# RWKV attention and a two-level mixture of experts: the routing's prefix product one step later, own bytes for the first part's buffers, the decay loaded as rows

## The chip, the cores and the metric

The kernel runs on one core of one Trainium2 chip, one launch. The metric is the device time of that core in microseconds (us). Engines are named as the profile names them: PE is TensorE's matmul stream and PEld its weight loads, DVE is VectorE, ACT is ScalarE, POOL is GpSimd, SP only issues DMAs here. "PEclk" or "clock" is the granted TensorE clock as a share of 2.4 GHz; it has two levels, 1.0 (2.4 GHz) and 0.5 (1.2 GHz).

## What is computed

Four batches of 8 heads, 768 positions, head size 48, all float32. First a linear recurrence over positions (RWKV), then every token goes to one of 16 experts in 4 groups of 4:

```python
for t in range(S):
    kt, vt, rt = k[:, :, t], v[:, :, t], r[:, :, t]
    cur = einsum('bhd,bhe->bhde', u * kt, vt)
    y[:, :, t] = einsum('bhd,bhde->bhe', rt, state + cur)
    state = w * state + einsum('bhd,bhe->bhde', kt, vt)
x = y.transpose(0, 2, 1, 3).reshape(3072, 384)
g_logits = x @ w_group;  g_idx = argmax(g_logits);  g_w = softmax(g_logits)[g_idx]
e_logits = x @ w_expert[g_idx];  e_idx = argmax(e_logits);  e_w = softmax(e_logits)[e_idx]
out = (g_w * e_w) * (relu(x @ w1[g_idx, e_idx]) @ w2[g_idx, e_idx])
```

## The kernel before

There are two parts that follow each other on PE: the recurrence with the routing, and the experts.

**First part.** The 768 positions are cut into 6 chunks of 128, so there are 24 tiles (chunk c, batch b), tile n = 4c + b, and 12 pairs of tiles g = n // 2. `load_pair` (L317) brings k, r and v of a pair from DRAM on SP's queue. A table of powers of the decay is built first (L125 to L158): `wc` from the loaded decay, four scans, a reciprocal, T1T, a transposition and a flip on PE, and T2. Then a software pipeline of steps s = 0 to 27 runs (L443), each step emitting for different tiles:

- `turn(s)` (L346): PE transposes r (`pr`) and scaled k (`pk`); DVE makes rT, ACT copies kT.
- `scores(s-1)` (L358): 8 products `pa` on PE, masked by DVE into `am`.
- `values(s-2)` (L372): products `py` and, except in the last chunk, `pu` on PE; DVE adds into `xt` and updates the state R (one operation in the first chunk, `ts` and R later).
- `rows_T(s-3)` (L411): PE transposes xt (`px`), ACT copies. `row_logits(s-4)` (L416): the routing's logits `pl` on PE, copied by ACT into `lg`.
- POOL: `scale_k` (L328, kh = k times T2) in even steps, `own` (L331, two products dg) in odd ones; DVE turns dg into the tile's own term in `own_values` (L337) in odd steps.

After tiles 3, 7, 11, 15 and 19 four tiles are routed together (the last four tiles as 2, 1 and 1). `route` (L202) gives four pieces: `choice` (DVE: maxima, one-hot `ohe`, running counts `cum`), `before` (PE: a prefix product `pre` of ohe with a triangle, and of cum with ones), `place_and_gate` (DVE) and `rows` (POOL: an indirect DMA of 128 rows into the expert's region of `x_sorted`). For tile n, emitted at the end of step s = n + 4, choice and before come in step s + 1 behind `rows_T` and ahead of `row_logits`, place_and_gate in s + 2, and one rows piece in each step from s + 2 on.

The order of PE, DVE, ACT and POOL is that of emission (`manual_schedule`, L434); each engine takes its instructions strictly in that order. SP's order is chosen by the scheduling framework. Tiles of a released pool give their bytes to later tiles, which then wait for the last use: the pool "powers" (L125) is released before "ring" and "wkv" (L299) are opened. PSUM has 8 banks given out in turn by `bank` (L74).

In step 2, ahead of its turn, come `late_constants` (L180: small DVE operations, some on one partition) and `zero_places` (L195: two DMAs of 2.7 MB each, issued from ACT's queue, that clear the regions). In step 4 both first experts' weights are asked for (L452).

**Second part** (L505 on): for each of 16 experts, 224 rows are read back from x_sorted, turned, multiplied by w1 and w2 on PE and written out by POOL. Nothing in it is changed.

Of the kernel before, what the change touches and what calls it, by code (L numbers as in the profile page):

```python
# [15 lines left out]
P = 128  # L16
# [10 lines left out]
def kernel(  # L27
# [58 lines left out]
    wcol = cst([P, HP], "wcol")  # L86
    nc.vector.memset(wcol, 1.0)
    for e in range(2):
        nc.scalar.dma_start(out=wcol[DP * e : DP * e + D, :], in_=w.rearrange("(a e) d -> e d a", e=2)[e])
# [6 lines left out]

    gw = cst([P, KO, NL], "gw")
    nc.scalar.dma_start(out=gw[:, :, 0:G], in_=moe_w_group.rearrange("(ko p) g -> p ko g", p=P))
    for g in range(G):
        nc.scalar.dma_start(  # L100
            out=gw[:, :, G + Eg * g : G + Eg * (g + 1)], in_=moe_w_expert[g].rearrange("(ko p) e -> p ko e", p=P)
        )
# [16 lines left out]
    )  # L119

# [4 lines left out]
    with tc.tile_pool(name="powers", bufs=1) as pw:  # L125

        wc = pw.tile([P, HP], FP32, name="wc")
        nc.vector.tensor_scalar(out=wc, in0=wcol, scalar1=W_LEAST, scalar2=W_MOST, op0=OP.max, op1=OP.min)
        none = pw.tile([P, P], FP32, name="none")
        nc.vector.memset(none, 0.0)  # L130

        up_to = pw.tile([P, HP, P], FP32, name="up_to")
        for hc in range(HP):
            nc.vector.tensor_tensor_scan(
                up_to[:, hc, :], wc[:, hc : hc + 1].to_broadcast([P, P]), none, 1.0, OP.mult, OP.add
            )
        by = pw.tile([P, HP], FP32, name="by")
        nc.vector.reciprocal(by, up_to[:, :, 64])
        for hc in range(HP):
            nc.vector.tensor_scalar(  # L140
                out=T1T[:, hc, :], in0=up_to[:, hc, :], scalar1=by[:, hc : hc + 1], scalar2=None, op0=OP.mult
            )
        ptab = bank([P, HP, P], "ptab")
        for hc in range(HP):
            nc.tensor.transpose(ptab[:, hc, :], T1T[:, hc, :], ident)
        tab = pw.tile([P, HP, P], FP32, name="tab")
        nc.scalar.copy(tab, ptab)
        ptab2 = bank([P, HP, P], "ptab2")
        nc.tensor.matmul(
            ptab2.rearrange("p a b -> p (a b)"), lhsT=flip, rhs=tab.rearrange("p a b -> p (a b)"), start=True, stop=True  # L150
        )
        nc.scalar.copy(
            T2.rearrange("p (a e) d -> p a e d", e=2), ptab2.rearrange("p a (e d) -> p a e d", e=2)[:, :, :, 0:D]
        )
        nc.vector.memset(WLm, 0.0)
        for e in range(2):
            rows = slice(DP * e, DP * e + D)
            nc.vector.tensor_copy(WLm[rows, :, D * e : D * (e + 1)], up_to[rows, :, P - 1 : P].to_broadcast([D, HP, D]))  # L158
# [10 lines left out]
    nc.vector.memset(nothing, 0.0)  # L169
# [9 lines left out]

    def late_constants():  # L180
# [4 lines left out]
        nc.vector.tensor_copy(cum[:, 0, :], start0)  # L185

# [8 lines left out]
    def zero_places():  # L195

        regions = xs_dram.rearrange("(e n) w -> n e w", e=GE)
        half = CAP // 2
        for j in range(2):
            nc.scalar.dma_start(out=regions[half * j : half * (j + 1)], in_=spread(nothing[0:half, :], 1, GE))  # L200

    def route(pool, lg, xt, T, sums, number, group):  # L202
# [43 lines left out]
        def place_and_gate():  # L246
            at = tl([P, T, GE], "at")
            nc.vector.tensor_mul(at, held["pre"], ohf)
            place = tl([P, T], "place")
            nc.vector.reduce_sum(out=place, in_=at, axis=AX)  # L250
            nc.vector.tensor_copy(place_i, place)
# [10 lines left out]

        def rows(i):
# [35 lines left out]
    with tc.tile_pool(name="ring", bufs=1) as ring, tc.tile_pool(name="wkv", bufs=2) as pool:  # L299
        R = [ring.tile([P, HP, 2 * D], FP32, name=f"R_{b}") for b in range(B)]  # L300
        RING = 4
        NP = NT // 2
        rts = [ring.tile([P, 2, H, DP], FP32, name=f"rt_{j}") for j in range(RING)]
        khs = [ring.tile([P, 2, H, DP], FP32, name=f"kh_{j}") for j in range(RING)]

        tiles = [(c, b) for c in range(NCH) for b in range(B)]
        kts, vts, dgs, dvs = {}, {}, {}, {}
        rkT, ams, xts, lgs, xTs = {}, {}, {}, {}, {}

        def load(src, g, dst):  # L310
            c, b0 = g // (B // 2), 2 * (g % (B // 2))
            nc.sync.dma_start(
                out=dst.rearrange("p a h d -> p (a h) d"),
                in_=src[b0 : b0 + 2, :, P * c : P * (c + 1), :].rearrange("b h t d -> t (b h) d"),
            )

        def load_pair(g):  # L317

            kts[g] = pool.tile([P, 2, H, D], FP32, tag="kt", bufs=3, name="kt")
            vts[g] = pool.tile([P, 2, H, D], FP32, tag="vt", bufs=5, name="vt")  # L320
            if g < RING:
                nc.vector.memset(rts[g][:, :, :, D:DP], 0.0)
                nc.vector.memset(khs[g][:, :, :, D:DP], 0.0)
            load(k, g, kts[g])
            load(r, g, rts[g % RING][:, :, :, 0:D])
            load(v, g, vts[g])

        def scale_k(g):  # L328
            nc.gpsimd.tensor_mul(khs[g % RING][:, :, :, 0:D], kts[g], spread(T2, 1, 2))  # L329

        def own(g):  # L331

            dg = dgs[g] = pool.tile([P, 2, H, D], FP32, tag="dg", name="dg")
            nc.gpsimd.tensor_mul(dg, rts[g % RING][:, :, :, 0:D], kts.pop(g))  # L334
            nc.gpsimd.tensor_mul(dg, dg, spread(ub, 1, 2))

        def own_values(g):  # L337
            du = pool.tile([P, 2, H], FP32, tag="du", name="du")
            nc.vector.reduce_sum(out=du, in_=dgs.pop(g), axis=AX)  # L339
            dv = dvs[g] = pool.tile([P, 2, H, D], FP32, tag="dv", bufs=3, name="dv")  # L340
            nc.vector.tensor_mul(dv, vts[g], spread(du, 3, D))
# [4 lines left out]
        def turn(n):  # L346
            g, a = n // 2, n % 2
            pr, pk = bank([P, HP, P], "pr"), bank([P, HP, P], "pk")
            for dst, src in ((pr, rts[g % RING]), (pk, khs[g % RING])):
# [22 lines left out]
        def values(n):  # L372
            c, b = tiles[n]
            g, a = n // 2, n % 2
            vt, kh = vts[g], khs[g % RING]
# [13 lines left out]
            if b == 0:  # L389
                xts[c] = pool.tile([P, B, XW], FP32, tag="xt", bufs=4, name="xt")  # L390
# [43 lines left out]
        engines = {mybir.EngineType.PE, mybir.EngineType.DVE, mybir.EngineType.Activation, mybir.EngineType.Pool}  # L434
        with tc.manual_schedule(engines=engines):
            load_pair(0)
            numbers()
            scale_k(0)
            load_pair(1)
            own(0)  # L440
            last_step = NT + 3
            todo = {}
            for s in range(last_step + 1):  # L443

                pieces = todo.pop(s, [])
# [13 lines left out]
                if 0 <= s - 1 < NT:  # L459
                    scores(s - 1)  # L460
# [354 lines left out]
```

## Time and profile before

| | us |
|---|---|
| median of 3 runs | 613.65 |
| lowest, highest | 612.9, 628.15 |
| the profiled execution, its own time | 611.63 |
| its span, first to last instruction | 609.9 |
| mean granted TensorE clock in it | 0.851 |
| PE busy | 549.3 (90%) |
| DVE busy | 187.3 (31%) |
| ACT busy | 85.6 (14%) |
| POOL busy | 126.5 (21%) |

How to read it: PE at half clock is as "busy" as at full clock, so the clock stands beside the busy share wherever it matters. A timeline row gives start, duration, engine, line, operation, what is written from what, the count of instructions merged into the row and, in brackets, how long the engine was idle before it and what released it. Durations of merged rows are from the first start to the last end, and matmuls' ends are modelled. "ACTq" and "SPq" rows are DMA issues: the time that the engine's queue spent on issuing.

### The profile page before, as it was taken

To read this page: it belongs to the slowest core of one execution; us is meant where nothing else is said; L and a number is where in the kernel's file an instruction comes from. 1 tells how busy PE (TensorE), PEld (TensorE's weight loads), DVE (VectorE), ACT (ScalarE), POOL (GpSimd) and SP (SyncE) were. 2 spreads that over 40 slices of the span, in tenths; PEclk is the share of its full clock that TensorE was granted. 3 is DMA by queue.
4 is the path that set the end of the run, shared out by engine and by line. 5 is a ranking of instruction groups with operands and counts; after the bars stand their busy time and mean duration, and the time that the engine had idled before them with its cause. 6 is when DMAs were issued, how large, how long until landed. Compare 5 with 4: busy or idle time off the path is not lost. (4 is left out here: it accounts for less than half of the span.)

```text
span 609.9 us, 7907 instructions
## 1 busy us (share of the span) xinstructions
PE 549.3 (90%) x3264; PEld 532.2 (87%) x3264; DVE 187.3 (31%) x484; ACT 85.6 (14%) x195; POOL 126.5 (21%) x102
## 2 busy tenths in 40 slices
PE   2679969899899899872999999999999999999993
PEld 0679859799799799872999999999999999999993
DVE  3576665742653643353011011111111011110100
ACT  1101101101110110110111111111111111111110
POOL 1836135505404311023010011101111011100111
PEclk9959967955955855555999999999999999999998
DMA  9999995523101001005246566564746556454200
GB/s 148 245 294 286 291 176 104 104 53 92 40 0 40 14 13 40 1 29 166 106 148 226 178 218 194 182 224 156 245 149 216 192 187 228 149 202 144 105 21 23
DMA packets 110989, 85.83 MB, mean 141 GB/s; under 512 B 78855, under 2 KB 102541, under 8 KB 110946
## 3 DMA queue, kind: packets, MB, share of 16 engines
q1 hardware_dynamic: 97344, 64.49, 40.1%
q10 hardware_dynamic: 10274, 11.30, 5.7%
q0 software_dynamic: 3328, 9.47, 4.5%
q8 instruction: 27, 0.44, 0.3%
q14 instruction: 16, 0.13, 0.1%
HBM read 70.25 MB, written 15.78 MB: 141 GB/s over the span
## 5 line engine op out<-in xcount | busy, mean ns | idle before, releaser
L543 PE MATMUL ph<-xe,w 128*128 128x224 f32 x768 | 152.2, 355 | 1.0 <-DVE xe L524 1.0
L556 PE MATMUL po<-hT,w 128*128 128x224 f32 x768 | 150.7, 353 | 0.0
L543 PEld LDWEIGHTS ph<-xe,w 128*128 128x128 f32 x768 | 145.4, 192 | 1.7 <-DVE xe L524 1.4
L556 PEld LDWEIGHTS po<-hT,w 128*128 128x128 f32 x768 | 144.2, 190 | 0.0
L573 POOL DMA_INDIRECT out_dram<-yt,ids x32 | 30.6, 957 | 292.7 <-DVE yt L568 287.8
L385 PE MATMUL py<-vt,am 128*128 128x48 f32 x384 | 71.6, 327 | 0.0
L385 PEld LDWEIGHTS py<-vt,am 128*128 128x128 f32 x384 | 69.1, 256 | 0.6 <-issue 0.2
L568 DVE TENSOR_SCALAR yt<-pb,gates 128x384 f32<-128x384 f32 (+1 forms) x32 | 18.2, 611 | 167.0 <-PE pb L566 167.0
L547 ACT ACTIVATE hT<-ph 128x448 f32<-128x448 f32 x64 | 34.8, 544 | 137.8 <-PE ph L543 137.8
L265 POOL DMA_INDIRECT x_sorted<-xt,place_i x24 | 24.2, 1007 | 122.3 <-DVE xt L261 117.8
L380 PE MATMUL py<-R,rT 128*128 128x96 f32 x160 | 46.0, 380 | 0.0
L365 PE MATMUL pa<-rT,kT 48*128 48x128 f32 x384 | 40.5, 370 | 4.6 <-DVE rT L353 4.6
L365 PEld LDWEIGHTS pa<-rT,kT 48*128 48x128 f32 x384 | 34.9, 266 | 10.5 <-issue 8.9
L370 DVE TENSOR_TENSOR am<-pa,later 128x512 f32<-128x512 f32 x48 | 30.9, 684 | 34.5 <-PE pa L365 34.5
L380 PEld LDWEIGHTS py<-R,rT 128*128 128x128 f32 x160 | 33.5, 259 | 3.2 <-issue 2.0
L559 ACT COPY yT<-po 128x224 f32<-128x224 f32 x48 | 16.6, 346 | 134.8 <-PE po L556 112.0
L524 DVE COPY xe<-px 128x448 f32<-128x448 f32 (+1 forms) x32 | 14.7, 502 | 65.0 <-PE px L521 65.0
L290 ACT COPY xT<-px 128x384 f32<-128x384 f32 x24 | 11.5, 480 | 152.4 <-PE px L289 152.4
L334 POOL TENSOR_TENSOR dg<-rt,kt 128x768 f32<-128x768 f32 x12 | 25.1, 2093 | 28.4 <-DVE du L339 20.8
L329 POOL TENSOR_TENSOR kh<-kt,T 128x768 f32<-128x768 f32 x12 | 21.9, 1829 | 32.1 <-DMA kt<-in_k_dram 19.9
L295 PEld LDWEIGHTS pl<-gw,xT 128*128 128x128 f32 x144 | 28.4, 286 | 0.0
L400 PE MATMUL pu<-vt,kh 128*128 128x96 f32 x160 | 28.2, 332 | 0.0
(93 smaller groups left out, 408.1 us busy)
## 6 DMA issues: line engine op xcount, KB each, us to landing
w<-in_moe_w_dram SPq DMA_DIRECT2D x32, 1536.0 KB, 6.5
x_sorted<-nothing ACTq DMA_DIRECT2D x2, 2702.0 KB
kt<-in_k_dram SPq DMA_DIRECT2D x12, 384.0 KB, 4.9
vt<-in_v_dram SPq DMA_DIRECT2D x12, 384.0 KB, 7.2
rt<-in_r_dram SPq DMA_DIRECT2D x12, 384.0 KB, 6.7
xg<-x_sorted ACTq DMA_DIRECT2D x16, 193.0 KB, 3.5
xg<-x_sorted ACTq DMA_DIRECT2D x16, 144.8 KB, 3.6
out_dram<-yt,ids POOLq DMA_INDIRECT x32, 2.5
```

The costliest lines, as they stand in the source:

```text
L265: ins = nc.gpsimd.indirect_dma_start(out=xs_dram, out_offset=bass.IndirectOffsetOnAxis(ap=place_i[:, i : i + 1], axis=0), in_=xt[:, i, :], ...
L295: nc.tensor.matmul(pl, lhsT=xT[:, ko, :], rhs=gw[:, ko, :], start=(ko == 0), stop=(ko == KO - 1))
L334: nc.gpsimd.tensor_mul(dg, rts[g % RING][:, :, :, 0:D], kts.pop(g))
L365: nc.tensor.matmul(pa[e][:, hc, :], lhsT=kT[rows, hc, :], rhs=rT[rows, hc, :], start=True, stop=True, skip_group_check=True,)
L370: nc.vector.tensor_mul(am[:, e], pa[e], spread(later, 1, HP))
L380: nc.tensor.matmul(py[:, hc, :], lhsT=rT[:, hc, :], rhs=R[b][:, hc, :], start=True, stop=False, skip_group_check=True,)
L385: nc.tensor.matmul(py[:, hc, D * e : D * (e + 1)], lhsT=am[:, e, hc, :], rhs=vt[:, a, 2 * hc + e, :], start=(c == 0), stop=True, skip_grou ...
L400: nc.tensor.matmul(pu[:, hc, :], lhsT=heads(kh, a, hc), rhs=heads(vt, a, hc), start=True, stop=True, skip_group_check=True,)
L543: nc.tensor.matmul(ph[:, i, :], lhsT=w1[:, ko, P * (f + i) : P * (f + i + 1)], rhs=xe[:, ko, :], start=(ko == 0), stop=(ko == KO - 1), ski ...
L547: nc.scalar.activation(hTs[e][:, f : f + 2, :], ph, AF.Relu)
L556: nc.tensor.matmul(po, lhsT=w2[:, fo, P * d : P * (d + 1)], rhs=hT[:, fo, :], start=(fo == 0), stop=(fo == FO - 1))
L573: ins = nc.gpsimd.indirect_dma_start(out=out, out_offset=bass.IndirectOffsetOnAxis(ap=ids, axis=0), in_=yt, in_offset=None, bounds_check=N ...
```

## The change

The change does these things:

1. **Routing.** `before` of the four-tile routings is emitted first thing in step s + 2, ahead of that step's turn; choice stays in s + 1. So `row_logits` of step s + 1 now stands ahead of `before` on PE. `place_and_gate` is split in two, gate first, then place.
2. **Bytes.** The pools "powers" and "ring" are gone: powers, ring, R, k and v tiles have bytes of their own in `const`. To make room, kh has 3 buffers (4 before), rT 3 (4), xt 3 (4), dv 2 (3); k has 4 (3).
3. **Head.** The decay is loaded as 4 partitions of contiguous rows (`w2h`) on SP's queue and turned by PE (`pw`), in place of two DMAs of single elements on ACT's queue. Loads come in the order r, k, v, and SP too is in the order of emission. A small ACT copy is put ahead of the table's. `scale_k(0)` is made half by DVE and half by POOL. The padding of the other ring tiles is cleared by POOL, in the head, not by DVE in steps. The gate weights `gw` (5 DMA issues on ACT) come behind T2, not ahead. WLm is made at the end of step 0.
4. **Steps.** `late_constants` moves to the end of step 2 and takes a memset; `zero_places` is split over steps 3 and 6; the first two experts' weights are asked for in steps 12 and 20; `scale_k` moves from even steps to the odd ones, just ahead of `own`.

The diff, cut to its core:

```diff
-    for e in range(2):
-        nc.scalar.dma_start(out=wcol[DP * e : DP * e + D, :], in_=w.rearrange("(a e) d -> e d a", e=2)[e])
+    rts = [cst([P, 2, H, DP], f"rt_{j}") for j in range(RING)]
+    khs = [cst([P, 2, H, DP], f"kh_{j}") for j in range(RING - 1)]
+    kts = [cst([P, 2, H, D], f"kt_{j}") for j in range(RING)]
+    vts = [cst([P, 2, H, D], f"vt_{j}") for j in range(RING + 1)]
+    nc.sync.dma_start(out=w2h[:, :, 0:D], in_=w.rearrange("(a e) d -> a e d", e=2))
...
+        load(r, g, rts[g % RING][:, :, :, 0:D])
+        load(k, g, kts[g % RING])
+        load(v, g, vts[g % (RING + 1)])
...
+    nc.scalar.copy(none[:, 0:1], ones[:, 0:1])
...
+    nc.tensor.transpose(pw, w2h.rearrange("p e d -> p (e d)"), ident[0:HP, 0:HP])
+    nc.vector.tensor_scalar(out=wc, in0=pw, scalar1=W_LEAST, scalar2=W_MOST, op0=OP.max, op1=OP.min)
...
     def late_constants():
...
+        nc.vector.memset(nothing, 0.0)
...
-        return choice, before, place_and_gate, rows
+        return choice, before, gate, place, rows
...
-            rT = pool.tile([P, HP, P], FP32, tag="rT", bufs=4, name="rT")
+            rT = pool.tile([P, HP, P], FP32, tag="rT", bufs=3, name="rT")
...
+        def piece_list(n):
+            choice, before, gate, place, rows = routing(n)
+            T = ROUTED[n]
+            if n >= NT - B:
+                lags = [0] * (4 + T)
+            else:
+                lags = [1, 2, 2, 2] + [3 + i for i in range(T)]
+            parts = [choice, before, gate, place] + [lambda i=i: rows(i) for i in range(T)]
+            return [(lag, part is before and lag > 0, part) for lag, part in zip(lags, parts)]
+        numbers()
+        scale_k(0, nc.vector, 0, 1)
+        scale_k(0, nc.gpsimd, 1, 2)
+        for t in rts[1:] + khs[1:]:
+            nc.gpsimd.memset(t[:, :, :, D:DP], 0.0)
+        load_small()
+        load_pair(1)
+        own(0)
...
+            if s in (3, 6):
+                zero_places(s // 6)
+            if s in (12, 20):
+                early[s // 20] = load_expert(s // 20)
+            for first, part in pieces:
+                if first:
+                    part()
             if s < NT:
                 turn(s)
-                    if s % 2 == 0 and s // 2 + 1 < NP:
-                        scale_k(s // 2 + 1)
-                    if s % 2 == 1 and s // 2 + 1 < NP:
-                        own(s // 2 + 1)
+                if s % 2 == 1 and s // 2 + 1 < NP:
+                    scale_k(s // 2 + 1, nc.gpsimd)
+                    own(s // 2 + 1)
...
+            for first, part in pieces:
+                if not first:
+                    part()
+            if s == 0:
+                state_decay()
+            if s == 2:
+                late_constants()
```

## Rows read from the trace of the kernel before

**Rows 1.** The page, part 2: TensorE's clock in 40 equal slices of the span, in tenths.
```profile
PEclk9959967955955855555999999999999999999998
```
**Rows 2.** Stretches between changes of clock: start:end, length, then busy time (instructions) of each engine, PEclk.
```profile
45.80:79.90 34.10, 29.31 (x287) 27.79 (x283) 23.61 (x36) 5.45 (x13) 15.76 (x9) 1.00 1.17 277
79.90:100.40 20.50, 18.60 (x99) 17.59 (x99) 10.31 (x26) 2.27 (x6) 3.38 (x3) 0.50 1.00 141
100.40:120.80 20.40, 17.99 (x171) 16.95 (x169) 15.11 (x28) 2.96 (x7) 14.32 (x9) 1.00 0.56 113
120.80:151.60 30.80, 30.61 (x163) 29.14 (x162) 11.80 (x28) 3.52 (x9) 8.49 (x6) 0.50 0.31 69
...
209.60:291.50 81.90, 65.34 (x320) 61.69 (x320) 32.10 (x137) 7.26 (x22) 11.74 (x12) 0.50 0.14 46
291.50:609.90 318.40, 309.03 (x1714) 307.05 (x1712) 37.10 (x110) 51.45 (x112) 30.61 (x32) 0.99 0.50 167
```
**Rows 3.** Timeline of PE: scores of tiles 6, 7, then 12 and 13.
```profile
63.22 1.16 PE L365 MATMUL pa<-rT,kT 48*128 48x128 f32 x16
...
69.88 1.16 PE L365 MATMUL pa<-rT,kT 48*128 48x128 f32 x16
...
124.63 2.08 PE L365 MATMUL pa<-rT,kT 48*128 48x128 f32 x16
...
137.23 2.08 PE L365 MATMUL pa<-rT,kT 48*128 48x128 f32 x16
```
**Rows 4.** Timeline around the prefix products of steps 8 and 12.
```profile
77.22 1.99 POOL L335 TENSOR_TENSOR dg<-dg,ub 128x768 f32<-128x768 f32 x1
77.73 1.58 DVE L223 TENSOR_TENSOR key<-lg,mx 128x80 f32<-128x80 f32 x1
...
81.80 0.69 PE L237 MATMUL pre<-ohe,later 128*128 128x64 f32 x2 [6.69 <-DVE ohe L229]
...
119.03 0.24 DVE L223 TENSOR_TENSOR key<-lg,mx 128x80 f32<-128x80 f32 x1
...
120.40 0.44 PE L237 MATMUL pre<-ohe,later 128*128 128x64 f32 x2 [2.41 <-DVE ohe L229]
...
121.50 1.41 PE L295 MATMUL pl<-gw,xT 128*128 128x20 f32 x6
```
**Rows 5.** Timeline of steps 2 to 4: late constants, scores of tiles 2 and 3.
```profile
30.48 2.04 DVE L189 TENSOR_TENSOR wlim<-wlim,wrow 1x384 f32<-1x384 f32 x1
...
34.19 2.58 PE L365 MATMUL pa<-rT,kT 48*128 48x128 f32 x16 [4.56 <-DVE rT L353]
...
44.41 1.78 PE L365 MATMUL pa<-rT,kT 48*128 48x128 f32 x16
```
**Rows 6.** Timeline of the head, from the first operations to the scores of tile 1.
```profile
0.90 0.24 POOL L172 IOTA iota_f<- 128x128 f32 x1 [0.40 <-POOLq L801]
...
3.49 4.43 ACTq L100 DMA_DIRECT2D gw<-in_moe_w_expert_dram  x4
...
7.42 0.17 DVE L128 TENSOR_SCALAR wc<-wcol 128x4 f32<-128x4 f32 x1 [5.36 <-DMA wcol<-in_w_dram]
...
13.62 0.48 ACT L152 COPY T<-ptab 128x384 f32<-128x384 f32 x1 [2.23 <-PE ptab L149]
...
18.61 1.82 POOL L334 TENSOR_TENSOR dg<-rt,kt 128x768 f32<-128x768 f32 x1 [2.62 <-DMA rt<-in_r_dram]
...
24.74 1.16 PE L365 MATMUL pa<-rT,kT 48*128 48x128 f32 x16
```
**Rows 7.** Timeline of the end of the first part: scores of tiles 22, 23, first rows of the last routings.
```profile
237.08 2.08 PE L365 MATMUL pa<-rT,kT 48*128 48x128 f32 x16
...
246.14 2.08 PE L365 MATMUL pa<-rT,kT 48*128 48x128 f32 x16
...
270.32 0.98 POOL L265 DMA_INDIRECT x_sorted<-xt,place_i  x1 [39.41 <-DVE xt L261]
```
**Rows 8.** The page, part 6: DMA issues, KB each, median us from issue to landing.
```profile
x_sorted<-xt,place_i POOLq DMA_INDIRECT x24, 2.8
```

More of the change, by code (lines that the diff above doesn't have):

```diff
@@ L95 @@
     nc.scalar.dma_start(out=wrow, in_=bass.AP(tensor=w.tensor, offset=w.offset, ap=[[0, 1], [1, H * D]]))
[L97 to L102, printed above, removed]
+    load_pair(0)
     ones = cst([P, P], "ones")
@@ L119 @@
     )
+    none = cst([P, P], "none")
+    nc.vector.memset(none, 0.0)
+    nc.scalar.copy(none[:, 0:1], ones[:, 0:1])
+    nc.vector.memset(none[:, 0:1], 0.0)
     T1T = cst([P, HP, P], "T1T")
@@ L124 @@
     WLm = cst([P, HP, 2 * D], "WLm")
[L125 to L135, printed above, removed]
-            )
[L137 to L158, printed above, removed]
@@ new lines @@
+    ptab = bank([P, HP, P], "ptab")
+    for hc in range(HP):
+        nc.vector.tensor_scalar(
+            out=T1T[:, hc, :], in0=up_to[:, hc, :], scalar1=by[:, hc : hc + 1], scalar2=None, op0=OP.mult
+        )
+        nc.tensor.transpose(ptab[:, hc, :], T1T[:, hc, :], ident)
+    tab = cst([P, HP, P], "tab")
+    nc.scalar.copy(tab, ptab)
+    ptab2 = bank([P, HP, P], "ptab2")
+    nc.tensor.matmul(
+        ptab2.rearrange("p a b -> p (a b)"), lhsT=flip, rhs=tab.rearrange("p a b -> p (a b)"), start=True, stop=True
+    )
@@ L178, in numbers, with state_decay @@
         nc.gpsimd.iota(region, pattern=[[RG, GE]], base=0, channel_multiplier=0, allow_small_or_imprecise_dtypes=True)
+    def state_decay():
+        nc.vector.memset(WLm, 0.0)
+        for e in range(2):
+            rows = slice(DP * e, DP * e + D)
+            nc.vector.tensor_copy(WLm[rows, :, D * e : D * (e + 1)], up_to[rows, :, P - 1 : P].to_broadcast([D, HP, D]))
     def late_constants():
@@ L244, in before, with gate @@
             )
[L246 to L251, printed above, removed]
+        def gate():
             sx = tl([P, T, NA], "sx")
@@ new lines @@
+        scale_k(0, nc.gpsimd, 1, 2)
[4 more added lines that the diff above has]
+        own(0)
+        todo = {}
+        early = {}
+        for s in range(NT + 4):
+            if s == NT + 2:
+                for t in sorted(todo):
+                    for _, part in todo.pop(t):
+                        part()
+            pieces = todo.pop(s, [])
+            if s % 2 == 0 and s // 2 + 2 < NP:
+                load_pair(s // 2 + 2)
+            if s in (3, 6):
[5 more added lines that the diff above has]
+                    part()
+            if s < NT:
+                turn(s)
+                if s % 2 == 1 and s // 2 + 1 < NP:
+                    scale_k(s // 2 + 1, nc.gpsimd)
+                    own(s // 2 + 1)
+            if 0 <= s - 1 < NT:
+                scores(s - 1)
+            if s % 2 == 1 and s // 2 < NP:
+                own_values(s // 2)
+            if 0 <= s - 2 < NT:
+                values(s - 2)
+            if 0 <= s - 3 < NT:
+                rows_T(s - 3)
+            for first, part in pieces:
+                if not first:
+                    part()
+            if s == 0:
+                state_decay()
+            if s == 2:
+                late_constants()
+            n = s - 4
+            if 0 <= n < NT:
+                row_logits(n)
+                if n in ROUTED:
+                    for lag, first, part in piece_list(n):
+                        if lag:
+                            todo.setdefault(s + lag, []).append((first, part))
+                        else:
+                            part()
@@ L488 @@
+        written.close()
     left_i = cst([1, 1], "left_i", I32)
```

141 lines of the change are left out of this document (58 added, 83 removed).

## Prediction

> **What bounds the kernel now.** I read the clock of the page first, because PE is busy 90% of the span and busy says nothing about speed. [Rows 1] show the two halves: up to about slice 19 the clock goes up and down between full (2.4 GHz) and half (1.2 GHz), behind that it is full. The stretches between changes [rows 2] put numbers to it: the experts, from 291.5 us on, run 318 us at 0.99 with PE busy 309 of them. Nothing there is changed, so I carry these 318 us over as they are. Everything is decided ahead of 291.5.
>
> In the first part PE sets the pace in both levels: a step, from the scores of one tile to those of the next, is 69.88 - 63.22 = 6.66 us at full clock and 137.23 - 124.63 = 12.6 us at half clock [rows 3]. DVE is busy 23.6 of 34.1 us in the full-clock stretch [rows 2], so it follows with room. A step at half clock thus costs 5.9 us more, and the reader should count such steps: of 270 us in the first part, the half-clock stretches of [rows 2] alone (20.5, 30.8 and 81.9, and one like the second, 165.2 to 195.9) make some 160.
>
> What brings the clock down is seen in the timeline around a prefix product [rows 4]. In step 12 PE has been idle for 2.41 us when `pre` starts at 120.40; it waits for DVE's `ohe`. The stretch at 1.0 ends at 120.8 [rows 2]. In step 8 the wait is 6.69 us and the clock falls within it. Every four-tile routing ends a full-clock stretch so. The clock came back after one whole cold step the first time (20.5 us), after two the second (30.8) and third time, and not at all after step 20 (81.9 us, to the experts). One more fall comes in the head: PE waits 4.56 us for an rT that stands behind the late constants on DVE [rows 5].
>
> **The change part by part.** The sum is made against the profiled execution's own 611.6 us; the median of the runs is 2.0 above it.
>
> *Head.* Today wc starts at 7.42, when the element-wise decay has landed; T2 is written at 13.62 + 0.48 = 14.10, 6.7 later [rows 6]. The new load is issued at about 0.8, first on SP. The trace has no load like it. Lower bound for landing: the 2.8 us of 128 indirect rows [rows 8]; upper bound: as late as today, gain nothing. It has 8 pieces in place of 384, so I take 3 us, and 0.5 for the turn on PE: wc at 4.3, T2 at 11.0. Tile 1's scores need the second pair's k scaled, and POOL's row now is: half of scale_k (0.9), six memsets, own(0) (two of 1.82 [rows 6]), scale_k(1) (1.82). A POOL memset of 256 columns isn't in the trace; an iota of 128 columns took 0.24 [rows 6], so 0.24 to 0.5, and I take 0.45, as it writes twice as much. That gives 11.0 + 0.9 + 2.7 + 3.6 + 1.8 = 20.0, and with turn(2)'s second half scores(1) at about 20.7 in place of 24.74: **-4.0** (bounds 0 and -7). own(0) waits no more for r, which today is loaded late (POOL waited 2.62 [rows 6]): r had to wait for the bytes of "powers". ACT's gate-weight issues (4.43 for four [rows 6], 4.8 with the fifth) now stand behind T2 and ahead of kT(0): kT at 16.5, scores(0) at 16.6. That is ahead of scores(1)'s own limit, hidden by POOL; without that cover it would cost the same 4.8.
>
> The Trainium skill, "DMA: Bandwidth & Descriptors", section "Anatomy of one DMA", gives about 2 us as the fixed part of a DMA; as an estimate by that page the decay is there 1 us sooner and the sum 1 us smaller. No row here shows it.
>
> *Late constants.* Their operations hold DVE for some 6 us (wlim alone 2.04 on one partition [rows 5]). Today PE needs rT(2) at once. At the end of step 2 they delay rT(3), which PE needs only after turn(3), scores(2) and values(1), about 5 us of work; with the memset added I expect a wait near 2.6 in place of 4.56: -2.0. Today tile 2's to tile 3's scores take 44.41 - 34.19 = 10.2 us at half clock [rows 5]; by the ratio 6.66/12.6 that is 5.4 at full clock: -4.8. Together **-6.8**, if the clock holds there; if it falls, +6 (bound). ACT's two zeroing issues move to steps 3 and 6; behind them wait kT and xT copies, needed a step later, so I cost them at nothing (cover: one step, 5.4 us or more; the trace's issues on ACT are 4.4 for four).
>
> *POOL beside choice.* In step 8 `key` took 1.58 while POOL ran dg (1.99), in step 12, with POOL idle, 0.24 [rows 4]; the wait of PE is 6.69 against 2.41. POOL was late in step 8 since its k, asked for behind the first expert weights, came late. With the weights asked for in steps 12 and 20 and the loads two pairs ahead, POOL finishes its 5.5 us (three products) ahead of choice, which is the last thing in the even steps: **-4.3**.
>
> *The prefix product.* What stands between its old and its new place on PE is only `row_logits`: six small matmuls. Choice still follows R on DVE, so PE still arrives early. I expect the wait to shrink from 2.41 by the 0.6 of row_logits at full clock, to 1.8. At half clock, where the work behind the pause runs today, row_logits took 1.41 [rows 4], some 1.2 of it PE's own: 4 pauses x 1.2 = **-4.8**. SP, POOL and ACT are not passed by it; gate and place lie behind, where today's piece lies.
>
> *Cold steps.* No row shows what PE does after a pause of 1.8 us: the shortest with work on both sides are the 2.41 of step 12 and the like, and each brought the clock down. Bounds: falls each time, or never. I take that it falls, since 1.8 is nearer to 2.41 than to no pause, and that it comes back after one cold step, as after step 8. PE now goes from the pause straight into turn and scores, with no row_logits between, so the work behind it is denser; this part is chosen, not shown. Then the second and third fall save one cold step each, 2 x 5.9 = **-11.8**. After step 20 the way from tile 21's to tile 23's scores is at full clock: 246.14 - 237.08 = 9.1 and a step of about 11 [rows 7], 20 us, by the ratio 6.66/12.6 11.3: **-8.7**.
>
> *End.* From tile 23's scores to the first POOL row are 270.32 - 246.14 = 24.2 us [rows 7]. Scores, two tiles' values and the logits in it are PE work at half clock, about 11 us; at full clock till the next pause I count **-5.0** (0 to -8). The eight rows' DMAs behind 270.32 and the read back are as they are.
>
> *Buffers.* Fewer kh, rT, xt and dv buffers are costed at nothing: kh's third-last user, values(2g-5), is a step and a half ahead of scale_k(g)'s need; rT, dv and xt are released a step or more ahead. Without that cover POOL's 5.5 us would come onto PE's path in each pair.
>
> Sum: 4.0 + 6.8 + 4.3 + 4.8 + 11.8 + 8.7 + 5.0 = 45.4; 611.6 - 45.4 = **566 us**.
>
> **Rivals.**
> *No fall.* A wait of 1.8 us doesn't bring the clock down. Then the four falls of the forecast go: each costs one cold step and about 2.5 us of the steps at its ends, 4 x 8.4 = 34: **532**. For it: PE's wait shrinks in each. Against: 2.41 was enough, in each case.
> *Clock as late as now.* Two cold steps after each fall, and none back after step 20. Then 11.8, 8.7 and most of the end's 5.0 are lost: **591**. For it: that is what the second to fourth fall did [rows 2].
> *POOL again beside choice.* POOL's products now come in one block of 5.5 us, and rows pieces order them behind DVE's place; if the block falls on choice, each of five pauses grows by the 4.3 that step 8 shows over step 12 [rows 4]: 566 + 21 = **588**. The Trainium skill, "SBUF — State Buffer", section "SBUF: two separate sides", says that POOL and a DVE operation with two SBUF inputs lock each other out for a whole instruction; the trace agrees (1.58 against 0.24), and by it this happens whenever the two meet. Against: DVE reaches choice a step after POOL can start.
> *Slower.* The clock, once down in step 8, never returns, as after 209.6, where tiles 20 to 23 were turned and scored without it. The seven steps that are warm today in the stretches from 100.4, 151.6 and 195.9 then cost 7 x 5.9 = 41 more, against 20 gained in the head, in steps 2 to 8 and by row_logits: **633**. It decides once there are four cold steps more than today.
>
> **How the numbers follow.** Forecast 0.40, no fall 0.27, clock as late as now 0.18, POOL 0.08, slower 0.05, in between or other 0.02. The likeliest is 566, by itself 555 to 575 (the head's bounds, a fall in step 4). The range of 8 in 10 goes from the no-fall case to the late clock, 530 to 592. Faster by over 2% (about what a measurement of this kernel tells from no change) means below 601: the first four cases, 0.93; within 2% 0.02, the rest; slower 0.05.
>
> **What would show it.** Scores of tile 1 near 20.7; wc near 4.3. PE's wait ahead of `pre` 1.8 us, with `pl` ahead of it. Half-clock stretches behind each `pre`, of about 20 us: shorter or none is the first rival, 30 and more the second. `key` and `oh` at 0.24, not 1.6. Experts' stretch 318 us. The forecast is wrong if the clock holds through the pauses, or if a buffer or a load stops POOL.

## The result, and the profile after

The changed kernel takes 579.1 us in the median of four executions (578.5 to 601.1), the kernel before beside it 613.3. The ratio is 0.9445, with a 95% interval from 0.942 to 0.947. The forecast was 566, so the direction held and the time lies in the range of 530 to 592, though outside the 555 to 575 that the likeliest case had by itself; 13 us of the 45 that the sum promised didn't come. Executions of one kernel differ here by how long the clock stays down, so each trace below is read against its own time: the main one took 579.6 us, and two others of the same kernel took 601.1 and 560.3.

First the page, part 2, of the 579.6 us execution: TensorE's clock in 40 slices, to be held against [rows 1].

```profile
PEclk9669955556958898559999999999999999999997
```

Then its stretches between changes of clock (start:end, length, then busy time and instructions of each engine, PEclk), against [rows 2].

```profile
17.70:38.10 20.40, 19.21 (x101) 18.10 (x102) 12.64 (x24) 1.65 (x3) 12.36 (x7) 0.50 1.21 241
38.10:72.30 34.20, 32.14 (x313) 30.49 (x312) 23.64 (x43) 6.35 (x16) 15.10 (x9) 1.00 1.03 219
72.30:140.50 68.20, 67.10 (x351) 63.70 (x349) 30.69 (x68) 6.93 (x17) 17.36 (x12) 0.50 0.48 113
140.50:161.00 20.50, 18.52 (x175) 17.66 (x173) 14.61 (x28) 2.96 (x7) 13.02 (x9) 1.00 0.75 201
161.00:178.10 17.10, 17.03 (x92) 15.92 (x92) 7.98 (x22) 2.16 (x6) 2.26 (x2) 0.50 0.16 61
178.10:198.60 20.50, 18.44 (x174) 17.65 (x174) 14.71 (x29) 2.96 (x7) 12.88 (x9) 1.00 0.08 31
...
225.90:260.00 34.10, 19.09 (x80) 17.83 (x79) 14.11 (x91) 2.27 (x10) 7.84 (x8) 0.50 0.27 88
260.00:577.90 317.90, 308.53 (x1711) 306.55 (x1710) 37.10 (x110) 51.34 (x112) 30.54 (x32) 0.99 0.50 168
```

The experts take 317.9 us as before. All of the gain lies ahead of them: the last stretch begins at 260.0 in place of 291.5. Besides the 20.4 us in the head and the 34.1 at the end, the reader should see two kinds of half-clock stretch behind the routings: one of 17.1 us, a single cold step, and one of 68.2 us, which runs over two routings. The timeline of the routing in step 8 answers [rows 4]. (A routing is named by the step of its choice; its `pre` now stands first in the step behind.)

```profile
68.38 0.74 PE L337 MATMUL pl<-gw,xT 128*128 128x20 f32 x6
...
69.58 0.24 DVE L263 TENSOR_TENSOR key<-lg,mx 128x80 f32<-128x80 f32 x1
...
71.05 0.41 PE L277 MATMUL pre<-ohe,later 128*128 128x64 f32 x2 [1.93 <-DVE ohe L269]
```

`key` takes 0.24 in place of 1.58, `pl` stands ahead of `pre`, and PE's wait is 1.93 in place of 6.69 (forecast 1.8). The clock falls at 72.3 all the same, and stays down.

What the clock costs can be read across the three executions of the changed kernel. The time at half clock is (1 - mean clock) x 2 x span: 192 us in the execution of 601.1, 150 in that of 579.6, 103 in that of 560.3. From the fastest to the slowest that is 40.8 / 89 = 0.46 us for each us at half clock (0.41 and 0.51 in the two halves of the way), an estimate from three executions. The kernel before has 182 us by the same formula, at 611.6. With 182 us the changed kernel would take about 579.6 + 32 x 0.46 = 594. So, by this estimate, of the 32 us that this execution is ahead some 17 come without the clock, and some 15 through 32 us less at half clock. The sum had 15 without the clock (head 4.0, late constants' wait 2.0, POOL 4.3, row_logits 4.8) and 30 through it (4.8 in step 3, 11.8, 8.7, 5.0). The first half of the sum came; of the second, about half did.

### The profile page after: what moved, and what is told of

It reads as the page before. It is cut to its first block, busy times and chain, and to the rows that moved or that the text cites. A ratio compares the mean times of both kernels' runs of the same rounds, so it can differ in the third digit from the quotient of the medians.

```text
span 599.3 us, 7905 instructions
## 1 busy us (share of the span) xinstructions
PE 554.4 (93%) x3265; PEld 537.5 (90%) x3265; DVE 185.1 (31%) x480; ACT 85.0 (14%) x196; POOL 124.5 (21%) x107
## 5 line engine op out<-in xcount | busy, mean ns | idle before, releaser
L404 PE MATMUL py<-vt,am 128*128 128x48 f32 x384 | 73.3, 333 | 0.9 <-DVE xt L411 0.9
L404 PEld LDWEIGHTS py<-vt,am 128*128 128x128 f32 x384 | 70.7, 262 | 1.7 <-DVE xt L411 1.1
L389 DVE TENSOR_TENSOR am<-pa,later 128x512 f32<-128x512 f32 x48 | 30.9, 685 | 33.9 <-PE pa L384 33.8
L594 ACT COPY yT<-po 128x224 f32<-128x224 f32 x48 | 16.6, 345 | 134.8 <-PE po L591 105.5
L348 POOL TENSOR_TENSOR kh<-kt,T 128x768 f32<-128x768 f32 (+1 forms) x12 | 21.4, 1784 | 59.2 <-PE pu L419 51.6
L419 PE MATMUL pu<-vt,kh 128*128 128x96 f32 x160 | 31.0, 356 | 0.0
L419 PEld LDWEIGHTS pu<-vt,kh 128*128 128x128 f32 x160 | 28.1, 263 | 0.0
L337 PEld LDWEIGHTS pl<-gw,xT 128*128 128x128 f32 x144 | 27.1, 274 | 0.0
```

The lines of the kernel that those rows point to most:

```text
L337: nc.tensor.matmul(pl, lhsT=xT[:, ko, :], rhs=gw[:, ko, :], start=(ko == 0), stop=(ko == KO - 1))
L348: engine.tensor_mul(khs[g % (RING - 1)][:, a0:a1, :, 0:D], kts[g % RING][:, a0:a1], spread(T2, 1, a1 - a0))
L389: nc.vector.tensor_mul(am[:, e], pa[e], spread(later, 1, HP))
L404: nc.tensor.matmul(py[:, hc, D * e : D * (e + 1)], lhsT=am[:, e, hc, :], rhs=vt[:, a, 2 * hc + e, :], start=(c == 0), stop=True, skip_grou ...
L419: nc.tensor.matmul(pu[:, hc, :], lhsT=heads(kh, a, hc), rhs=heads(vt, a, hc), start=True, stop=True, skip_group_check=True,)
```

## The experiments

My theory after the result: the pause ahead of `pre` brings the clock down, and after step 8 the clock doesn't come back within one cold step. Rivals: the length of the cold stretch is a matter of the rest of the change (loads, late constants, POOL), or the pauses are not what matters.

**The same kernel again.** No edit (the label is `after_again`; this and the next three share the runs of the kernel before, 606.7).

> The changed kernel once more, for a trace of its usual time (578.5 to 579.5 us in three of its four runs; the one profile there is of a run of 601.1 with one half-clock stretch of 81.9 us from 38.4 on). Both theories: 578 to 580 us. Theory A (each prefix product's wait drops the clock, which comes back after one cold step): half-clock stretches of about 17 us that begin at the pre of steps 12, 16 and 20, and one in the head that is shorter than 82 us. Theory B (the clock's falls have nothing to do with these waits): stretches that begin elsewhere.

Measured: 576.3 us (560.3 to 578.7), a little below the 578 to 580 of both theories. In the profiled execution, of 560.3 us, the clock holds through the wait of step 8 and falls at that of step 12. The timeline of both, with an earlier wait of 0.95 us, then the stretches around them:

```profile
36.36 1.99 PE L404 MATMUL py<-vt,am 128*128 128x48 f32 x16 [0.95 <-DVE xt L411]
...
67.85 0.41 PE L277 MATMUL pre<-ohe,later 128*128 128x64 f32 x2 [1.93 <-DVE ohe L269]
...
97.34 0.54 PE L277 MATMUL pre<-ohe,later 128*128 128x64 f32 x2 [1.93 <-DVE ohe L269]
```

```profile
29.20:97.50 68.30, 63.37 (x618) 60.29 (x618) 53.49 (x102) 12.21 (x29) 32.89 (x19) 1.00 1.03 243
97.50:114.50 17.00, 17.00 (x93) 15.94 (x92) 8.25 (x23) 2.16 (x6) 1.87 (x2) 0.50 0.44 79
114.50:135.00 20.50, 18.57 (x177) 17.73 (x175) 14.75 (x28) 2.95 (x7) 13.58 (x9) 1.00 0.71 204
135.00:152.10 17.10, 16.97 (x92) 15.82 (x91) 8.11 (x22) 2.16 (x6) 2.13 (x2) 0.50 0.17 61
```

One instruction with one wait of 1.93 us, twice, and the clock falls only the second time. So the size of the wait alone doesn't decide whether the clock falls. Where it falls here, it is back after 17 us (the forecast had about 20). Theory A's places, steps 12, 16 and 20, are where it falls.

**The pause taken away.** `before` keeps its lag of two steps, but stands behind rows_T of step s + 2, not first in it.

```diff
-            return [(lag, part is before and lag > 0, part) for lag, part in zip(lags, parts)]
+            return [(lag, False, part) for lag, part in zip(lags, parts)]
```

> The prefix product is emitted behind rows_T of its step, with gate and place, no longer ahead of the turn: DVE's choice is a whole step old by then, so PE doesn't wait. Theory A: no fall at a routing; each of four falls cost about 5.9 us of one cold step and 2.5 at its ends, and the wait itself 1.9, so 4 x 10 = 40 less: about 540 us (530 to 552), clock at 1.0 from the head's last fall to the end of the first part. Theory B: only the waits go, 5 x 1.9: about 569 us, half-clock stretches stay.

Measured: 523.1 us (522.0 to 525.4), 53 us under the changed kernel beside it, ratio to before 0.862 (0.857 to 0.866). Theory A's direction holds, but its range of 530 to 552 is missed: falls and waits cost more than the 40 us that it gave them. The stretches:

```profile
17.20:30.90 13.70, 11.76 (x66) 10.88 (x68) 8.09 (x14) 1.17 (x2) 11.53 (x7) 0.50 1.29 184
30.90:177.70 146.80, 144.37 (x1410) 138.25 (x1407) 125.02 (x262) 27.27 (x71) 68.69 (x43) 1.00 0.65 165
177.70:201.60 23.90, 9.57 (x39) 8.57 (x38) 10.12 (x71) 1.27 (x5) 7.84 (x8) 0.50 0.38 124
201.60:520.30 318.70, 309.32 (x1716) 307.36 (x1714) 37.09 (x110) 51.45 (x112) 30.57 (x32) 0.99 0.49 167
```

From 30.9 to 177.7 PE runs at full clock without a break, through the four-tile routings of steps 8 to 24, whose `pre` costs it no wait. The time at half clock is 43 us, 107 less than in the 579.6 us execution. 107 x 0.46 = 49, and the five waits ahead of `pre` in that execution (1.93, 1.10, 1.93, 1.93 and 1.31) are 8: together about the 57.6 us between the two spans. So the pauses and the time at half clock make the whole difference, by this estimate. Not all of it is the routing's: the head's stretch, which this edit doesn't touch, is 13.7 us here and 20.4 there, some 3 us by the 0.46.

**The pause filled.** 12 transposes of the identity, whose result nothing reads, ahead of each four-tile `pre`.

```diff
+            if T == TG:
+                fill = bank([P, 4, P], "fill")
+                for i in range(12):
+                    nc.tensor.transpose(fill[:, i % 4, :], ident, ident)
```

> The order of the changed kernel, with 12 transposes of the identity (result unused) on PE ahead of each four-tile prefix product, about 1.4 us of work at full clock: PE's order and DVE's chain are kept, PE's pause is filled with work that computes nothing. Theory A: the clock holds, four falls of 8.4 us go, the wait's time stays: about 547 us (538 to 560), though PE does more. Theory B: no gain, 579 us or up to 5 us more.

Measured: 548.2 us in the median, 28 under the changed kernel, but in two pairs: 534.6 and 537.3, 559.1 and 559.2. The timeline around step 16's `pre` in an execution of 537.3:

```profile
126.42 0.74 PE L341 MATMUL pl<-gw,xT 128*128 128x20 f32 x6
127.01 1.51 PE L279 MATMUL fill<-ident 128*128 128x128 f32 x12
...
129.00 0.43 PE L281 MATMUL pre<-ohe,later 128*128 128x64 f32 x2 [0.48 <-DVE ohe L269]
```

`pre` starts no sooner with respect to `pl` (2.6 us behind it; in the changed kernel's step 8 it is 2.7): DVE is as late as ever. Only PE's idleness is gone, 0.48 left of 1.93, and that alone is worth 28 us in the median (17 to 42 by the pair). So it is the idleness that costs, not the waiting. The Trainium skill, "TensorE: Matmul & The Clock Gate", section "HAM oscillation — how this bites in real kernels", names idle gaps of PE as the cause in the same way; its example has waits of 3 to 5 us, and here 1.93 was enough. The execution of 537.3 has 51 us at half clock, in the head and at the end only, and 1.00 from 37.3 to 190.9 through all five `pre`; that is 8 us more at half clock than with the late place, 4 us by the 0.46. From one `pre` to the next it takes 29.5 us in place of 27.1, 2.4 for each pause and fill, which makes the rest of its distance to 523. It also stands near the 532 that the rival "no fall" gave. Of the two near 559 only the mean clock is known, 0.911: some 99 us at half clock. Where it fell in them isn't known, so that the fill holds the clock each time isn't shown.

**The routing edit undone.** The changed kernel with the old lags (choice and before in s + 1, ahead of row_logits).

```diff
-                lags = [1, 2, 2, 2] + [3 + i for i in range(T)]
+                lags = [1, 1, 2, 2] + [3 + i for i in range(T)]
-            return [(lag, part is before and lag > 0, part) for lag, part in zip(lags, parts)]
+            return [(lag, False, part) for lag, part in zip(lags, parts)]
```

> Of the change the routing's part alone undone: choice and prefix product again in one step, ahead of row_logits; the rest as changed. Theory A: wait 2.4 to 2.6 us in place of 1.9, row_logits behind it at half clock (1.2 us each), and as before two cold steps after a fall: 5 + 2 to 3 x 5.9, 590 to 600 us. Theory B: 0.6 us for each of five waits, about 582 us.

Measured: 597.0 us (591.8 to 601.8), ratio 0.980 (0.972 to 0.988). Its stretches behind the routings of steps 8, 12 and 20:

```profile
69.90:97.20 27.30, 27.30 (x148) 25.86 (x147) 11.23 (x25) 3.07 (x7) 8.54 (x6) 0.50 0.70 190
110.80:141.60 30.80, 30.71 (x162) 29.09 (x164) 11.96 (x29) 3.52 (x9) 8.36 (x6) 0.50 0.32 66
...
199.60:281.50 81.90, 65.21 (x319) 61.52 (x320) 32.64 (x138) 7.25 (x22) 11.75 (x12) 0.50 0.14 46
```

By the medians the routing edit is worth 597.0 - 576.3 = 20.7 us within the change, the rest of the change 606.7 - 597.0 = 9.7. With the old place the long stretch after step 20 is there again, 81.9 us to the us as in [rows 2].

**The changed kernel a third time.** No edit, one execution; it is the one shown in the result.

> The changed kernel a third time, one look, to see the clock's stretches of one more execution. Theory A as it now stands (a wait of 1.93 us drops the clock in most places, not in all; the time is set by how much of the first part runs at half clock): a time near 576 to 579 us with some 140 us at half clock, against 103 us in the execution of 560.3 and 192 in that of 601.1; 0.46 us of time for each us at half clock. Theory B (the time differs for another reason): no such relation.

Measured: 579.6. It and the next three share the runs of the kernel before, 613.0.

**The routing edit alone**, on the kernel before: `before` first thing in step s + 2.

```diff
+                for piece in firsts.pop(s, []):
+                    piece()
...
+                                if i == 1:
+                                    firsts.setdefault(s + 2, []).append(piece)
+                                else:
+                                    todo.setdefault(s + 1 + max(0, i - 1), []).append(piece)
-                                todo.setdefault(s + 1 + max(0, i - 1), []).append(piece)
```

> The kernel before with the routing's edit alone: the prefix product first in step s + 2, behind row_logits. Theory A (the routing's edit carries most of the gain, as its undoing in the changed kernel cost 597.0 - 576.3 = 21 us): 580 to 592 us beside a kernel before of 606 to 613. Rival C (head and steps carry it, and the edit needs them): 600 us or more. Half-clock stretches after the prefix products of 17 us, in place of 30.7.

Measured: 592.7 us (570.4 to 598.0), ratio 0.971 (0.955 to 0.987), just outside theory A's 580 to 592. The medians lie 20.3 us apart, as much as inside the change, and with the 9.7 for the rest they make the 30 of the whole. But the interval runs from 8 to 28 us and one execution is 43 ahead, so that the two parts simply add isn't shown.

**The late place alone**, on the kernel before: `before` behind rows_T of step s + 2.

```diff
-                                todo.setdefault(s + 1 + max(0, i - 1), []).append(piece)
+                                todo.setdefault(s + 1 + min(i, 1) + max(0, i - 2), []).append(piece)
```

> The kernel before with the prefix product emitted behind rows_T of step s + 2, ahead of row_logits: no wait for choice. Theory A: from the head's last fall (45.8) on the clock holds to the end of the first part; the head and the late constants stay, worth about 11 us at tile 3's scores, so 523 + 11 to 18 = 534 to 541 us. Rival C: the clock falls also for other reasons there (POOL beside choice in step 8), 555 us or more.

Measured: 549.2 us (535.1 to 550.0): 64 us from one line, twice the whole change. One of the four executions lies in theory A's 534 to 541, the others between it and rival C. In the execution of 549.5 one fall is left in the middle, and the timeline shows whence:

```profile
73.33 1.82 POOL L329 TENSOR_TENSOR kh<-kt,T 128x768 f32<-128x768 f32 x1 [14.57 <-DMA kt<-in_k_dram]
...
76.20 1.59 DVE L223 TENSOR_TENSOR key<-lg,mx 128x80 f32<-128x80 f32 x1
...
77.78 1.80 POOL L335 TENSOR_TENSOR dg<-dg,ub 128x768 f32<-128x768 f32 x1
77.83 1.85 DVE L224 TENSOR_TENSOR key<-key,desc 128x80 f32<-128x80 f32 x1
...
79.98 1.81 DVE L228 TENSOR_TENSOR oh<-key,kx 128x80 f32<-128x80 f32 x1
...
83.46 0.51 PE L237 MATMUL pre<-ohe,later 128*128 128x64 f32 x2 [1.64 <-ACT lg L296]
```

```profile
83.70:114.40 30.70, 30.70 (x164) 29.16 (x163) 18.52 (x32) 3.82 (x10) 15.99 (x10) 0.50 0.90 152
114.40:203.20 88.80, 86.83 (x840) 83.05 (x838) 72.16 (x171) 15.86 (x43) 34.11 (x23) 1.00 0.21 51
```

POOL had waited 14.57 us for k, so its three products fall on choice, DVE's two-input operations take 1.6 to 1.85 in place of 0.24, and even the late `pre` waits 1.64, for ACT's copy of `lg`, which stood behind an ACT operation that had waited 7.34 us for DVE's `ex`. This is the contention that the change takes away in step 8. The Trainium skill, "SBUF — State Buffer", section "SBUF: two separate sides", tells of this lock; these rows agree.

**Head, first try: k of the second pair scaled sooner.** pre_late, with scale_k(1) ahead of own(0) on POOL, for the 3 us that PE waits for kh in the head (below).

```diff
+        scale_k(1, nc.gpsimd)
         own(0)
...
-                    scale_k(s // 2 + 1, nc.gpsimd)
+                    if s > 1:
+                        scale_k(s // 2 + 1, nc.gpsimd)
```

> The changed kernel with the prefix product behind rows_T of its step and, in the head, scale_k(1) ahead of own(0) on POOL: it takes away the 3.4 us in which PE waits for the second pair's kh at 19, where the first half-clock stretch (13.7 us from 17.2 on) begins. Theory A: 3.4 us of wait and half of 13.7 us go: 523.1 - 8 = 515 us (512 to 520). Rival: own(0) then comes 1.8 us later, du and rT(2) behind it on DVE, and the wait only moves there: 521 to 525 us.

Measured: 538.0 us (522.3 to 617.0), no gain: theory A is out, and the median is worse than the rival's 521 to 525 too. The waits moved. The timeline of the execution of 531.0:

```profile
23.60 1.16 PE L384 MATMUL pa<-rT,kT 48*128 48x128 f32 x16 [1.49 <-DVE rT L372]
...
32.46 0.63 PE L370 MATMUL pk<-ident,kh 128*128 128x128 f32 x4 [2.44 <-POOL kh L348]
```

PE's wait for the second pair's kh is 1.42 (at 16.64) in place of 3.39, but then it waits 1.49 for rT behind own(0)'s DVE work, and 2.44 for the third pair's kh; the clock is at half from 26.5 to 29.9 and from 33.3 to 57.2. What the execution of 617.0 met isn't known.

**Head, second try: the wait filled.** pre_late, with 28 transposes of the identity (result unused) between `pr` and `pk` of turn(2).

```diff
+                if n == 2 and dst is pk:
+                    fill = bank([P, 4, P], "fill")
+                    for i in range(28):
+                        nc.tensor.transpose(fill[:, i % 4, :], ident, ident)
```

> The kernel with the prefix product behind rows_T (523 us, 520.3 of span), with 28 transposes of the identity (result unused) on PE in step 2 between pr and pk, where PE waits 3.4 us for POOL's kh and the clock falls (half from 17.2 to 30.9). The wait stays, PE's pause is filled. Theory A (a pause of PE, not the wait behind it, drops the clock): the 13.7 us of half clock go or start later, 523 - 6 = 517 us (514 to 520). Theory B (the clock there falls for something else): 523 to 527 us, the stretch from 17 to 31 stays.

Measured: 566.0 us (525.3 to 592.3), outside both theories; one execution of the four, 525.3, lies in theory B's. (This and the next share a before of 612.8.) The first fall is gone, but the execution of 590.3 shows a later one, and what it costs. Timeline, then stretches:

```profile
31.54 0.63 PE L374 MATMUL pk<-ident,kh 128*128 128x128 f32 x4 [2.18 <-POOL kh L348]
...
34.96 3.65 PE L408 MATMUL py<-vt,am 128*128 128x48 f32 x16 [1.17 <-DVE xt L415]
```

```profile
34.30:184.50 150.20, 149.54 (x773) 142.89 (x773) 65.94 (x128) 14.99 (x38) 43.72 (x27) 0.50 0.55 125
```

PE is busy for 149.5 of 150.2 us, and at half clock for all of them. No pause of PE keeps it there.

**The expert weights early again.** pre_late with both experts' loads asked for in step 4, as before the change.

```diff
-            if s in (12, 20):
-                early[s // 20] = load_expert(s // 20)
+            if s == 4:
+                for e in range(2):
+                    early[e] = load_expert(e)
```

> The same kernel with both first experts' weights asked for in step 4, as in the kernel before, in place of steps 12 and 20; everything else as there. Theory A: pair loads then stand behind 6.3 MB, POOL's products come late and fall beside choice in step 8: key and oh 1.6 to 1.8 us in place of 0.24; PE has a step of slack for it now, so 523 to 528 us where the clock holds, and 14 more (the 549 against 535 of the kernel before with the prefix product late) where it falls. Rival: SP runs ahead far enough that the pair loads don't suffer: key 0.24, 523 us.

Measured: 523.3 us in the median (522.8 to 546.6), as pre_late. Two of the six executions took 540.5 and 546.6; in the traced one, of 546.6, the clock fell at 38.5, behind a wait of 0.95 us, and stayed at half for 54.6 us. `key` in all eight routings of it (min/median/max in ns):

```profile
L263 DVE TENSOR_TENSOR key<-lg,mx x8: 178/241/245, 89.1 to 209.6; 128x80 f32<-128x80 f32 x5, 128x20 f32<-128x20 f32 x2, 128x40 f32<-128x40 f32 x1
```

It never meets POOL. My prediction said that asking for these loads later takes POOL off the choice; this run shows that it isn't needed for that. With own bytes and SP in the order of emission, SP asks for the pairs well ahead anyway; which of these two does it wasn't tried apart.

**The late constants later.** pre_late, `late_constants` at the end of step 6, its memset in step 0.

```diff
+        nc.vector.memset(nothing, 0.0)
...
-        nc.vector.memset(nothing, 0.0)
...
-            if s == 2:
+            if s == 6:
                 late_constants()
```

> The kernel with the prefix product behind rows_T (523 us), with late_constants at the end of step 6 and not of step 2 (the memset of the zeros for the regions, which the zeroing DMAs need, at the end of step 0). In steps 3 to 5 DVE is late by the 3 to 6 us of these operations, and PE waits 1.0 us for xt or 2.2 us for kh at 31 to 38; in four kernels the clock fell there in some executions, for 24 to 150 us. Theory A: without them DVE isn't late there and no such fall comes: 519 to 524 us in every run. Rival (POOL's products, which are behind since the head, bring the same waits): 520 to 525 in some runs, 540 and more in others.

Measured: 523.0 us (520.4 to 525.4), ratio 0.858 (0.851 to 0.865): no difference to pre_late. Theory A's 519 to 524 holds but for one execution, of 525.4; pre_late had no fall in these steps in its one traced execution either, so this run alone decides nothing. (This and the next share a before of 612.6.)

**Both.** late_consts6 with the 28 transposes.

> The same, with the 28 transposes that fill PE's pause in the head (their kernel took 525, 542, 590 and 592 us, the clock falling at 34). Theory A: neither the head nor steps 3 to 5 drop the clock: 515 to 519 us in every run. Rival: POOL's products come late for turn(4), PE waits 2 us for kh at 31, the clock falls there in some runs: 540 us and more.

Measured: 517.0 us (516.6 to 517.5), ratio 0.847 (0.841 to 0.853), the best of all and with the least spread. Its wait at turn(2) and its stretches:

```profile
15.16 3.22 PE L372 MATMUL fill<-ident 128*128 128x128 f32 x28
...
19.01 0.66 PE L374 MATMUL pk<-ident,kh 128*128 128x128 f32 x4 [0.63 <-POOL kh L348]
```

```profile
12.90:169.90 157.00, 155.40 (x1520) 148.27 (x1518) 135.60 (x271) 29.39 (x74) 83.90 (x54) 1.00 0.79 175
169.90:197.20 27.30, 13.02 (x48) 11.80 (x49) 12.01 (x81) 1.55 (x7) 7.84 (x8) 0.50 0.33 109
```

Full clock from 12.9 to 169.9. It is 6 us under late_consts6 beside it, and every execution of the one is under every one of the other. Neither edit gains this alone: in the traced execution with the fill alone the clock falls at the waits behind the late constants (2.18 and 1.17 above), and with the constants moved those two waits are gone; the 0.63 at turn(2) is PE's only wait for kh.

## Why the prediction was right or wrong

**Head, right, with a term of its working mis-sized and one fall not foreseen.** Timeline of the 579.6 us execution, against [rows 6]:

```profile
4.08 0.16 DVE L158 TENSOR_SCALAR wc<-pw 128x4 f32<-128x4 f32 x1 [0.70 <-PE pw L156]
...
10.21 0.48 ACT L179 COPY T<-ptab 128x384 f32<-128x384 f32 x1 [2.23 <-PE ptab L176]
10.66 2.17 ACTq L190 DMA_DIRECT2D gw<-in_moe_w_expert_dram  x4
...
12.07 0.81 POOL L469 MEMSET rt<- 128x256 f32 x3
...
14.08 1.23 PE L384 MATMUL pa<-rT,kT 48*128 48x128 f32 x16
...
18.89 1.11 PE L370 MATMUL pk<-ident,kh 128*128 128x128 f32 x4 [2.99 <-POOL kh L348]
19.93 2.08 PE L384 MATMUL pa<-rT,kT 48*128 48x128 f32 x16
```

The decay landed some 2.7 us after its issue (w2h issued at 1.07, `pw` released at 3.81), near the 3 us taken. The Trainium skill, "DMA: Bandwidth & Descriptors", section "Anatomy of one DMA", gives the 2 us that the prediction quotes for a DMA that GpSimd issues; this load was issued on SP's queue. wc starts at 4.08 (forecast 4.3), T2 stands at 10.69 (11.0), the scores of tile 1 come at 19.93 (20.7; 24.74 before): -4.8 for -4.0. The gate weights' issues took 2.17 for four in place of 4.43 [rows 6], so scores(0) stands at 14.08, not 16.6; a memset took 0.27, not 0.45. What I didn't see: by my own chain PE has nothing to do between turn(2)'s `pr` and POOL's kh. That wait is 2.99 us, the clock falls at 17.7 and stays down for 20.4 us. I had costed POOL's row as a delay and not as idleness of PE.

**Late constants, right in one execution.** In that of 601.1 the scores of tiles 2 and 3 lie 5.14 us apart (5.4 forecast; 10.2 before [rows 5]), and the wait behind them is 0.95 us (2.6 forecast). In that of 579.6 the head's fall covers them, and tile 3 comes at 38.47 in place of 33.70:

```profile
28.56 1.16 PE L384 MATMUL pa<-rT,kT 48*128 48x128 f32 x16
...
33.70 1.16 PE L384 MATMUL pa<-rT,kT 48*128 48x128 f32 x16
...
35.82 0.42 PE L404 MATMUL py<-vt,am 128*128 128x48 f32 x2 [0.95 <-DVE xt L411]
```

The last row stands where I had put a bound (+6 if the clock falls there), but the fall is far dearer: behind a wait of 0.95 the clock fell at 38.5 and stayed down for 81.9 us, PE busy 80.8 of them. At 0.46 that is 38 us, of which one cold step behind step 8, which lies in it, would have made 8. The same wait of 0.95 in the execution of 560.3 left the clock up. This is the stretch of the execution of 601.1:

```profile
38.50:120.40 81.90, 80.80 (x422) 76.88 (x420) 32.87 (x64) 8.83 (x22) 20.02 (x13) 0.50 0.65 154
```

**POOL beside choice: right in effect, wrong in reason.** `key` takes 0.24 in all routings, and the rival that had it again falls. The reason that I gave, expert weights moved to steps 12 and 20, falls with the run that moved them back; what did it, own bytes or SP's order, is open.

**Prefix product: right.** The wait is 1.93 (1.8 forecast), `pl` stands ahead.

**Cold steps: the step that failed.** The prediction said: it falls each time, and "comes back after one cold step". The first half holds at most pauses, the second at the later ones: 17.1 us behind step 16 in the execution of 579.6, and 17.0 or 17.1 behind 12, 16 and 20 in that of 560.3 (in that of 601.1 behind 12 and 16, and 27.3 behind 20). Behind step 8 of the first it is 68.2 us, through the pause of step 12. Two stretches of 17.1 would be 34 there; the other 34 us at 0.46 are 16 us. The head's 20.4 us add 9. Together 25, more than the 13 missing. On the other side the clock was down for only 3.4 us behind step 20, 14 us less (6 by the 0.46), and the terms without the clock brought some 2 us more than forecast; that leaves 17 for 13, and the last 4 I can't place. The rival "no fall" was what one wait of 1.93 did in step 8 of one execution; the rival "clock as late as now" describes the first half of the routings in another. The forecast lay between them for the wrong reason: it took one length of stretch for all, where the length differs by place and execution. That the time lies in the range owes something to luck: one of the four executions, that of 601.1, is outside it.

**End: right.** From tile 23's scores to the first POOL row are 237.23 - 218.60 = 18.6 us, 5.6 less than [rows 7] (5.0 forecast). (In the term ahead of it, after step 20, 20 us times 6.66/12.6 is 10.6 and not 11.3, so the working's own sum is 565; nothing hangs on it.)

```profile
218.60 1.16 PE L384 MATMUL pa<-rT,kT 48*128 48x128 f32 x16
...
237.23 0.98 POOL L307 DMA_INDIRECT x_sorted<-xt,place_i  x1 [22.84 <-DVE place_i L303]
```

**Buffers: right.** POOL does wait for kh's buffer, until PE's `pu` has read it (42.4 us in all in the 579.6 us execution), but off the path: PE waits for kh only once, in the head.

**Not settled.** Why the clock comes back after 17 us in one place and after 68, 82 or 150 in another, with PE equally busy, and which waits bring it down. In the three traces of the changed kernel ten waits of 1.93 or 1.94 came at full clock: nine stand ahead of a fall, one doesn't. All three of 1.31 or 1.32 in step 24 do, and of two of 0.95 one does. No run here tells what decides. What the runs do tell: with these waits gone (filled_consts6) the clock holds from the head to the last routings.

## What to carry to other kernels

A pause of PE costs what the clock does afterwards, not its own length: look at each wait of one to three us that PE has in the middle of dense work, and move the waiting instruction behind work that is ready, or, where there is none, fill the gap. To shorten a pause gains less than to remove it: here 2.4 to 1.9 us gave 20 us, and to none another 53. When one wait is taken away, look for the next on the same path before counting the gain: two edits in the head of which neither gained by itself gave 6 us together.

## What the runs showed of the hardware that I had not expected

- The clock stays at half for 68, 82 and 150 us while PE is busy for 98 to 99.6% of them.
- Waits of 0.95, 1.31 and 1.93 us were each the last idleness ahead of a fall; others of 0.95 and of 1.93, at the same instructions, were not.
- Transposes whose result is unused can keep the clock up: with 28 of them in the head (and the late constants moved) it is at 1.00 from 12.9 to 169.9 us, without them, in the traced execution of late_consts6, it was at half from 20.4 to 27.2.
- A us at half clock costs 0.46 us in the changed kernel, by three executions. The step times of [rows 3] give about the same: 1 - 6.66/12.6 = 0.47.
